# Transposes of q and k right behind the product of the first half pair, with a new order of the whole attention stage

## The chip, the cores and the metric

The kernel runs on one core of one Trainium2 chip. The metric is device time in microseconds (us), the median of several executions, lower is better. A profile is one more execution, recorded by the hardware. Five engines run side by side, each taking its own instructions in order: TensorE (PE, with its weight loads as PEld), VectorE (DVE), ScalarE (ACT), GpSimd (POOL) and SyncE (SP), which here only issues DMAs. Matrix products land in PSUM, eight banks of 512 float32 columns in each of 128 partitions.

## The reference

Attention in which a query sees only the keys of its own hash bucket, followed by a gated MLP:

```python
q_bits = (einsum(q, proj) > 0); k_bits = (einsum(k, proj) > 0)       # 6 bits each
mask   = q_bucket[:, :, :, None] == k_bucket[:, :, None, :]
scores = where(mask, (q @ k.T) / sqrt(64), -1e9); scores -= scores.max(-1)
x      = softmax(scores) @ v                 # batch 4, heads 8, seq 768, head_dim 64
h = gelu(x @ w_in); u, w = split(h); w = layernorm(w) * g_ln
out = x + (u * (w_sg @ w + b_sg)) @ w_out    # seq 768, d_model 512, d_ff 1024
```

## The kernel before

The 32 heads are worked on as 16 pairs: two heads of 64 rows fill the 128 partitions. The attention stage takes the pairs one after the other, and each pair in two halves of 384 queries. The MLP follows from about 422 us on. The numbers inside are float32; a product that must be exact is split into a high and a low part.

For a pair, the work on PE is made of these groups; the letter is used in the rest of the text.

- **T** (line 544, `parts`): six 128x128 transposes of q, and six of k, into a slot of two PSUM banks each. ACT copies each slot back over the raw tile (line 556, "x"), then makes the rounded part hq or hk (line 550, "hi"), and DVE the rest lq or lk (line 553, "lo"). The raw tiles have one buffer each, so the next pair's load waits until these are through. The T of pair n+2 are made while pair n is worked on.
- **F** (line 576): projections that give the hash bits of pair n+2. DVE takes their sign, and four DMAs put them into the tiles fq and fk.
- **M** (line 622, `largest`): 128 query rows against half of the keys, to find the largest score; four matmuls. DVE reduces the two banks to a maximum (line 627, "R"). Six M make a half.
- **S** (line 640, `shift`): three small transposes of the maxima, which ACT copies into a row of fq (line 646, "C", two copies per half). S and C are made one half ahead of the scores that use them.
- **W** (line 662, `weigh`): 128 keys against the 384 queries of a half, eight matmuls into a two-bank slot. ACT takes the exponential into a tile p (line 667, "E"). Six W make a half. POOL adds the p tiles up (line 676).
- **U** (line 716) sums over partitions, and **V** (line 692, `weighted`) is the product of six p tiles with v, 24 matmuls. ACT copies the result out (line 707, "un").

M and W use the array in two halves of 64 rows at once ("row"); U and F use it by 32 columns, V by 64 columns; T and S use it whole.

PE's order is not the order of the code. Each group is put down with an engine, an estimated cost and a priority (`Plan.add`). A planner (`Plan.order`) plays the engines through with its own costs and takes, when an engine is free, the ready group with the lowest priority number; PSUM slots are handed out on the way. The constants at the top and the table SHAPE shift the priorities, so changing them reorders every engine, and with it the slot that a group gets. A group whose slot was used before waits until the engine that reads the earlier contents is through. At most four two-bank slots exist, and U, V, F and S take single banks of the same eight.

Of the kernel before, what the change touches and what calls it, by code (L numbers as in the profile page):

```python
# [18 lines left out]
DRAM = bass.MemoryType.DRAM  # L19


MLP = {"xl": "POOL", "gm": "DVE", "gl": "POOL", "wg": 456.91, "wo": -41.91, "x": 458.24}

NSUM = 3
BANKED = False
HID = 304.61
AVP = 3.07
S0P = -1.32
AHEAD = 4
PREP, SHIFTP, FINP, WSTEP, WP = 10.15, -4.79, 9.31, 9.56, 22.97  # L30
LOADS = "SP"
GPLACE = 4
XLATE = 5.15
FIRST = -5
RXP = 9.55
FEAT = 2.68
LOWP = 7.25
LOADP = 2.29
LATF = 3.2
OM = [0.01, 0.27, 0.0, 2.44, 0.37, 0.0, -1.25, 0.68, 0.49, 1.13, -0.06, 0.0]  # L40
OW = [0.0, 0.2, 0.0, 0.29, 0.0, 0.0, 0.0, 0.0, -0.69, 0.48, 0.0, 1.07]
# [4 lines left out]
OH = [2.49, 0.0]  # L46
OT = [1.05, 0.73]
OF = [1.53, -2.21]
RATE = 2.72
WFROM = 1.22  # L50
ADDW = 2


SHAPE = {"A": [0.62, -1.19, 0.62, -0.38, 0.62, 1.31, 0.62, -1.1, 0.62, 0.62, 0.62, 0.62, -0.96, 0.62, 0.62, 0.62, 0.62, -2.07, 0.62, 0.62], "AV": [0.04, 0.0], "C": [3.79, 2.41, 3.53, 3.52], "E": [0.0, 0.0, -1.65, -0.24, 1.16, 0.0, -0.63, 2.51, 0.36, 0.0, -2.01, 0.0], "M": [0.0, 0.0, 0.0, 0.0, 0.0, -0.21, 0.0, 0.0, 0.0, -0.91, 0.0, -1.94], "R": [0.6, 0.6, 1.13, 0.6, -0.6, 0.6, 0.6, 0.44, 0.6, -1.08, 0.6, 0.6], "S": [0.18, 1.75], "T": [0.47, 0.68], "W": [0.0, 0.0, 0.0, 0.0, 0.0, 0.0, 0.0, 0.0, 0.0, 0.0, 0.0, 0.0], "hi": [3.88, -3.27], "lo": [0.0, -1.87], "m": [1.19, -3.45], "rc": [-3.68, 1.0], "sm": [4.69, -0.03], "un": [2.6, 6.46], "xt": [7.81, 0.51], "F": [-1.53], "sg": [-3.33], "x": [0.35, 1.9]}


class Plan:
# [46 lines left out]
    def add(self, engine, cost, prio, fn, r=(), w=(), dma=0, port=None, form=None, lat=0.0, tag=None):  # L104

        port = engine == "POOL" if port is None else port
        if tag in SHAPE:
            i = self.count[tag] = self.count.get(tag, -1) + 1
            prio += SHAPE[tag][i % len(SHAPE[tag])]
        if engine == "DVE" and port:  # L110
# [165 lines left out]
def kernel(  # L276
# [16 lines left out]
    nc = tc.nc  # L293

    B, H, S, D = q.shape
    P = 128
    NT = S // P
    HT = NT // 2
    SH = S // 2
# [112 lines left out]
    PE, DVE, ACT, POOL, SP = "PE", "DVE", "ACT", "POOL", "SP"  # L412
    xs = [dram.tile([DM, S], F32, name=f"xs_{b}") for b in range(B)]

    plan = Plan()
# [59 lines left out]
    if True:  # L475
# [5 lines left out]
        def ps_two():  # L481
            ps_s.list.append(plan.slot(ps_slots, 2, lambda i: psb[:, i:i + 2, :]))
            return ps_s.list[-1]
# [50 lines left out]
            st.ft = [f_tile(s, n % 2) for s in range(2)]  # L534
            return st

        def parts(st, s, prio):

            hh, lo, raw, fac, tp = st.hi[s], st.lo[s], st.raw[s], (SCALE, 1.0)[s], ps_two()

            def tr():
                for hf in range(2):
                    for i in range(HT):
                        nc.tensor.transpose(tp()[:, hf, i * P:(i + 1) * P],  # L544
                                            raw()[:, hf * HT + i].rearrange("p j d -> p (j d)"), ident)

            scale, fac = (fac, 1.0) if not st.n else (1.0, fac)

            def high():
                nc.scalar.mul(hh(), x_of(raw), fac)  # L550

            def low():
                nc.vector.scalar_tensor_tensor(lo(), x_of(raw), fac, hh().bitcast(F32), op0=ALU.mult, op1=ALU.subtract)

            plan.add(PE, 0.654, prio, tr, [raw], [tp], tag="T")
            plan.add(ACT, 0.81, prio, lambda: nc.scalar.mul(x_of(raw).rearrange("p (a b) -> p a b", a=2), tp()[:, :, :SH], scale), [tp], [raw], tag="x")
            def split(p1, p2):
                plan.add(ACT, 0.81, p1 + OH[s], high, [raw], [hh], tag="hi")
                if not st.n:
                    plan.add(POOL, 1.88, p2 + OL[s], lambda: nc.gpsimd.tensor_sub(lo(), x_of(raw), hh().bitcast(F32)), [raw, hh], [lo])  # L560
                    return
                plan.add(DVE, 0.98, p2 + OL[s], low, [raw, hh], [lo], port=True, tag="lo")

            st.split.append(split)

        def x_of(raw):
            return raw().rearrange("p t j d -> p (t j d)")
# [115 lines left out]
        def weighted(st, hf, prio, owed, nxt=None):  # L683

            av, p, v_ = ps_one(), st.p, st.v
            half = Pair()
            half.n, half.b, half.hp, half.hf, half.av, half.sum = st.n, st.b, st.hp, hf, av, st.sum

            def product():
                for kt in range(NT):  # L690
                    for j in range(2):
                        nc.tensor.matmul(av()[row(j), :SH + 1], v_()[:, j, kt, :], p[kt]()[:, j, :], start=(kt == 0), stop=(kt == NT - 1))  # L692

            if owed is None:
                plan.add(PE, 1.3 * HT, prio, product, p + [v_], [av], form="col")
            else:
                sums, tp = owed.sum, ps_one()

                def sumup():
                    total(sums, tp)  # L700
                    if nxt:
                        nxt.project()

                plan.add(PE, 0.35 + (0.66 if nxt else 0.0), prio - 0.02, sumup, p[-1:] + [sums] + (nxt.raw if nxt else []), [tp] + ([nxt.fp] if nxt else []), form="col32")
                plan.add(PE, 1.3 * HT, prio - 0.01, product, p + [v_], [av], form="col", tag="AV")
            half.un = un = late.ring([P, SH + 1], F32, "un", 3)
            plan.add(ACT, 0.48, prio - 1, lambda: nc.scalar.copy(un(), av()[:, :SH + 1]), [av], [un], tag="un")  # L707
            if owed is not None:
                finish(owed, tp, prio)
            return half  # L710
# [35 lines left out]
        NPAIR = B * NP  # L746
        sts = {}

        def prepare(n, prio):
            sts[n] = st = load(n, prio + LOADP)  # L750
            for s in range(2):
                parts(st, s, prio + 0.1 * s + OT[s])

        def loadv(st, prio):
            n = st.n
# [5 lines left out]
        def rest(st, prio):  # L761
            if st.n:
                st.sign(prio + OF[0])
                scatter(st, prio + OF[1])
            for s, f in enumerate(st.split):
                f(prio + XLATE + 0.1 * s, prio + LOWP + 0.1 * s)
            loadv(st, prio - 8)

        def maxima(i):
            n, t = divmod(i, NT)  # L770
            if n >= NPAIR:
                return
            p0 = 2 * (i - AHEAD) + S0P
            largest(sts[n], t, p0)
# [3 lines left out]
        owed = None  # L778
        for n in range(2):
# [3 lines left out]
            else:  # L783
                for s in range(2):
                    direct(sts[n], s, FIRST + 0.1 * s)
            rest(sts[n], (-12, -3)[n] + 0.3)
# [7 lines left out]
        for n in range(NPAIR):  # L794
            for c in range(NT):
                if c == 0 and n + 2 < NPAIR:
                    prepare(n + 2, 2 * (g_ := NT * n) + PREP)
                hf, k0, g = c // HT, 2 * (c % HT), NT * n + c
                maxima(g + AHEAD)
                weigh(sts[n], hf, k0, 2 * g)  # L800
                if c % HT == HT - 1:
                    nxt = sts.get(n + 2) if hf else None
                    if nxt:
                        features(nxt, 0, True)
                    owed = weighted(sts[n], hf, 2 * g + AVP + OA[hf], owed, nxt)
                    if nxt:
                        rest(nxt, 2 * g + FEAT)
                if c == 1 and GPLACE <= n < GPLACE + NT:
                    t = n - GPLACE
                    for h in range(P // Q):  # L810
                        c0 = t * P + h * Q
                        dma(2 * g + 20, 0.6, cost=0.85, fn=lambda eng, t=t, h=h, c0=c0: eng.dma_start(  # L812
                            wgd[t][h * Q:(h + 1) * Q].rearrange("b (f a) -> b f a", a=Q),
                            w_sg[:, c0:c0 + Q].rearrange("(f b) a -> b f a", b=Q)), r=[ticks[-1]], w=[(wgdb, (t, h))])
                while conv and WFROM + RATE * conv[0][0] <= 2 * g:
                    at_, job, args = conv.pop(0)
                    job(plan, w_tile, *args, 2 * g + WP, after=[ticks[-1]])
# [3 lines left out]

    M_ = MLP
    b1, b2 = Pool("b1", "right"), Pool("b2", "right")
# [160 lines left out]
    for b in range(B):  # L984
        p = 500 + 1000 * b
# [43 lines left out]
```

## Time and profile before

| | |
|---|---|
| three runs, us | 727.96, 728.36, 728.73 (median 728.36) |
| the profiled execution, us | 727.57 |
| its span, first to last instruction | 725.8 |
| granted TensorE clock over the span | 1.000 |
| busy share PE, DVE, POOL, ACT | 99%, 73%, 59%, 52% |

The profiled execution lies 0.79 us under the median of the three, and 1.8 us of it lie outside its span. A busy PE is not a PE that never waits: the ends of matmuls are modelled, and a wait of a tenth of a microsecond between two groups shows as a later start rather than as idle time. So the starts of successive groups are read here, not the busy share.

### The profile page before, as it was taken

The numbers are of one execution on the slowest core, as the hardware profiler recorded it, in microseconds if no ns is written. First come the engines' busy times: TensorE is split into PE (matmuls) and PEld (weight loads), VectorE is DVE, ScalarE is ACT, GpSimd is POOL, SyncE is SP. The second block draws the span as 40 slices with busy tenths as digits, with TensorE's granted clock in tenths as the row PEclk, the third lists the DMA queues.
The fourth block names the chain that finished last, engine by engine and source line by source line (L and its number), as shares of the span: only waits on it lengthen the run. The fifth ranks groups of instructions, "written<-read, shape, count | busy, mean of one in ns | idle before, by whom it ended". The sixth has DMA issues, their size and how long they took to land.

```text
span 725.8 us, 14083 instructions
## 1 busy us (share of the span) xinstructions
PE 715.9 (99%) x5294; PEld 565.4 (78%) x5294; DVE 528.9 (73%) x781; ACT 380.2 (52%) x611; POOL 430.9 (59%) x294
## 2 busy tenths in 40 slices
PE   8999999999999999999999999999999999999997
PEld 4676766767677676777767669988999899988995
DVE  6887788888998988888888359455953595349533
ACT  2675666657656565765656547422661275117410
POOL 4678787787877777596777848540562056304230
PEclk9999999999999999999999999999999999999999
DMA  6333652673665355346442236815130511051004
GB/s 130 85 66 92 149 119 87 133 155 100 151 150 138 96 111 140 87 126 156 103 113 60 60 113 193 174 39 119 30 88 29 116 30 45 15 131 30 0 1 117
DMA packets 177765, 70.38 MB, mean 97 GB/s; under 512 B 157728, under 2 KB 167968, under 8 KB 177696
## 3 DMA queue, kind: packets, MB, share of 16 engines
q1 hardware_dynamic: 176464, 68.62, 39.7%
q10 hardware_dynamic: 1232, 0.86, 0.5%
q8 instruction: 42, 0.69, 0.4%
q14 instruction: 27, 0.22, 0.1%
HBM read 51.61 MB, written 17.24 MB: 95 GB/s over the span
## 4 chain that ended last, share of the span: by engine, by line
PE 93%; DVE 3%; SPq 1%; DMA 1%; ACT 1%; issue 1%; DVEq 0%; ACTq 0%
PE psb L662 18%; PE psb L692 16%; PE psb L937 14%; PE psb L888 9%; PE psb L919 9%; PE psb L966 9%; PE psb L622 8%; PE psb L544 3%; DVE mx L627 2%; PE psb L716 2%; PE psb L576 1%; PE psb L640 1%; PE psb L455 1%; SPq L812 1%; DMA w<-in_moe_w_in_dram 0%
## 5 line engine op out<-in xcount | busy, mean ns | idle before, releaser
L676 POOL TENSOR_TENSOR sum<-sum,p 128x768 f32<-128x768 f32 x128 | 225.6, 1762 | 82.2 <-ACT p L667 74.5
L627 DVE TENSOR_REDUCE mx<-psb 128x2 f32<-128x768 f32 x192 | 175.9, 949 | 40.3 <-PE psb L622 38.5
L667 ACT ACTIVATE p<-psb 128x768 f32<-128x768 f32 x192 | 148.9, 814 | 29.4 <-PE psb L662 20.7
L692 PE MATMUL psb<-p,v 128*64 128x385 f32 x768 | 131.2, 491 | 0.0
L692 PEld LDWEIGHTS psb<-p,v 128*64 128x64 f32 x768 | 52.3, 137 | 71.7 <-issue 62.7
L662 PE MATMUL psb<-hq,hk 64*128 64x384 f32 x384 | 72.1, 371 | 1.1 <-DVE mx L627 0.6
L622 PE MATMUL psb<-fk,fq 64*128 64x384 f32 x384 | 66.9, 343 | 1.5 <-DVE mx L627 1.0
L676 POOL TENSOR_TENSOR sum<-p,p 128x768 f32<-128x768 f32 x32 | 61.2, 1914 | 11.7 <-ACT p L667 11.6
L622 PE MATMUL psb<-hk,hq 64*128 64x384 f32 x384 | 65.1, 333 | 0.0
L662 PE MATMUL psb<-lq,hk 64*128 64x384 f32 x384 | 65.0, 333 | 0.0
L662 PE MATMUL psb<-fq,fk 64*128 64x384 f32 x384 | 64.9, 333 | 0.0
L662 PE MATMUL psb<-hq,lk 64*128 64x384 f32 x384 | 64.8, 332 | 0.0
L948 POOL TENSOR_TENSOR gs<-gt,gs 128x384 fp32r<-128x384 f32 x32 | 33.6, 1054 | 52.0 <-ACT gs L945 47.2
L937 PE MATMUL psb<-wgh,zh 128*128 128x384 f32 x192 | 64.1, 334 | 0.0
L937 PE MATMUL psb<-wgl,zh 128*128 128x384 f32 x192 | 64.1, 334 | 0.0
L937 PE MATMUL psb<-wgh,zl 128*128 128x384 f32 x192 | 64.1, 334 | 0.0
L898 POOL TENSOR_TENSOR mv<-mv,epsr 128x1 f32<-128x1 f32 x24 | 13.2, 549 | 85.2 <-DVE mv L897 65.7
L872 ACT ACTIVATE h<-psb 128x384 f32<-128x384 f32 (+1 forms) x56 | 29.2, 534 | 65.8 <-PE psb L888 60.3
L707 ACT COPY un<-psb 128x385 f32<-128x385 f32 x32 | 15.4, 481 | 90.1 <-PE psb L692 90.1
L966 PE MATMUL psb<-woh,gs 128*128 128x512 f32 x192 | 59.9, 389 | 0.0
L873 DVE SCALAR_TENSOR_TENSOR h<-h,psb 128x384 f32<-128x384 f32 (+1 forms) x56 | 32.9, 603 | 28.4 <-ACT h L872 28.3
L940 DVE TENSOR_TENSOR gt<-psb,b_bc 128x384 f32<-128x384 f32 x32 | 17.8, 555 | 47.3 <-PE psb L937 43.7
(122 smaller groups left out, 1552.7 us busy)
## 6 DMA issues: line engine op xcount, KB each, us to landing
q<-in_q_dram SPq DMA_DIRECT2D x32, 192.0 KB
v<-in_v_dram SPq DMA_DIRECT2D x16, 384.0 KB
rs<-r SPq DMA_DIRECT2D x64, 96.0 KB
xs<-xt SPq DMA_DIRECT2D x32, 192.0 KB
x<-xs SPq DMA_DIRECT2D x16, 384.0 KB
rx<-xs SPq DMA_DIRECT2D x96, 64.0 KB
out_dram<-ob SPq DMA_DIRECT2D x24, 256.0 KB
k<-in_k_dram SPq DMA_DIRECT2D x31, 192.0 KB
```

Source lines behind the costliest of these rows:

```text
L622: nc.tensor.matmul(sc[kh]()[:, j, :SH], x[0]()[row(j), qs], x[1]()[row(j), kh * SH:(kh + 1) * SH], start=(n == 0), stop=(n == 1))
L627: plan.add(DVE, 0.95, prio + OM[2 * t + kh], lambda kh=kh: nc.vector.tensor_reduce(mx()[:, i, :, kh], sc[kh]()[:, :, :SH], axis=AX.X, op=A ...
L662: nc.tensor.matmul(sc[i]()[:, j, :SH], x()[row(j), ks], y()[row(j), cs], start=(n == 0), stop=(n == 3))
L667: plan.add(ACT, 0.81, prio, lambda i=i: nc.scalar.activation(p[i]()[:, :, :SH], sc[i]()[:, :, :SH], AF.Exp), [sc[i]], [p[i], ticks[-1]], t ...
L676: plan.add(POOL, 1.88, prio + 0.6, lambda i=i, first=first: nc.gpsimd.tensor_add(sums(), (first or sums)()[:, :, :SH], p[i]()[:, :, :SH]), ...
L692: nc.tensor.matmul(av()[row(j), :SH + 1], v_()[:, j, kt, :], p[kt]()[:, j, :], start=(kt == 0), stop=(kt == NT - 1))
L873: plan.add(DVE, us + 0.07, prio, lambda: nc.vector.scalar_tensor_tensor(h2()[:, :n], h2()[:, :n], 1.0 / GA, ps()[:, :n], op0=ALU.add, op1= ...
L888: nc.tensor.matmul(ps(), x()[:, ts_], w[:, c, FH:FF], start=(c == 0 and n == 0), stop=(c == NC - 1 and n == 2))
L919: nc.tensor.matmul(ps()[:, :SH], w[:, c, fs], x()[:, cs], start=(c == 0 and n == 0), stop=(c == NC - 1 and n == 2))
L937: nc.tensor.matmul(vp()[:, :SH], z()[:, t, fs], w()[:, t, cs], start=(t == 0 and n == 0), stop=(t == NT - 1 and n == 2))
L948: nc.gpsimd if e == POOL else nc.vector).tensor_sub(gl()[:, cs], gt(), gh()[:, cs].bitcast(F32)),
L966: nc.tensor.matmul(po(), a()[:, ts_], w()[:, f, :], start=(f == 0 and n == 0), stop=(f == NF - 1 and n == 2))
```

## The change

The T of q and k no longer belong to `prepare` (except for the first two pairs). They are put down in the main loop right behind the product V of a pair's first half, and a marker buffer, written by V and read by T, forbids them to come earlier. Constants and SHAPE have new values, and with them the order of all engines. Line numbers behind the first edits move by 1 to 7; line 662 becomes 663, 622 becomes 623, 544 becomes 545.

```diff
-HID = 304.61
+HID = 266.96
+TP = -6.37
-PREP, SHIFTP, FINP, WSTEP, WP = 10.15, -4.79, 9.31, 9.56, 22.97
+PREP, SHIFTP, FINP, WSTEP, WP = 2.53, -5.4, 9.46, 2.63, 22.15
...
-        def parts(st, s, prio):
+        def parts(st, s, prio, behind=()):
...
-            plan.add(PE, 0.654, prio, tr, [raw], [tp], tag="T")
-            plan.add(ACT, 0.81, prio, lambda: nc.scalar.mul(x_of(raw).rearrange("p (a b) -> p a b", a=2), tp()[:, :, :SH], scale), [tp], [raw], tag="x")
+            plan.add(PE, 0.654, prio, tr, [raw, *behind], [tp], tag="T")
+            plan.add(ACT, 0.81, prio + (OT[s] - TP if behind else 0.0), lambda: nc.scalar.mul(x_of(raw).rearrange("p (a b) -> p a b", a=2), tp()[:, :, :SH], scale), [tp], [raw], tag="x")
...
-                plan.add(PE, 1.3 * HT, prio - 0.01, product, p + [v_], [av], form="col", tag="AV")
+                half.mark = plan.buf("mark", 1000)
+                plan.add(PE, 1.3 * HT, prio - 0.01, product, p + [v_], [av, half.mark], form="col", tag="AV")
...
             sts[n] = st = load(n, prio + LOADP)
-            for s in range(2):
-                parts(st, s, prio + 0.1 * s + OT[s])
+            if n < 2:
+                for s in range(2):
+                    parts(st, s, prio + 0.1 * s + OT[s])
...
                     if nxt:
                         rest(nxt, 2 * g + FEAT)
+                    elif not hf and n + 2 < NPAIR:
+                        for s in range(2):
+                            parts(sts[n + 2], s, 2 * g + TP + 0.1 * s, [owed.mark])
```

PE in the program before, the tenth pair, from the end of V of its first half (p and v are V's operands, identr and m those of S, the rest W and M):

```order
L692 MATMUL psb<-p_160,v_2880 64x385 x2
L640 MATMUL psb<-identr,m_71 66x128 x3
L662 MATMUL psb<-hq_4_2853,hk_4_2832 128x384 x2
L662 MATMUL psb<-hq_4_2853,lk_4_2864 128x384 x2
L662 MATMUL psb<-lq_4_2882,hk_4_2832 128x384 x2
L662 MATMUL psb<-fq_177,fk_178 128x384 x2
L622 MATMUL psb<-fk_176,fq_175 128x384 x2
L622 MATMUL psb<-hk_5_3144,hq_5_3168 128x384 x2
```

Here S follows V at once, then the first W and M. Some 20 rows later on PE before, the two T (operand ident) stand between an M and a W:

```order
L622 MATMUL psb<-fk_176,fq_175 128x384 x2
L622 MATMUL psb<-hk_5_3144,hq_5_3168 128x384 x2
L544 MATMUL psb<-ident,k_3198 128x128 x6
L544 MATMUL psb<-ident,q_3213 128x128 x6
L662 MATMUL psb<-hq_5_3168,hk_5_3144 128x384 x2
L662 MATMUL psb<-hq_5_3168,lk_5_3178 128x384 x2
```

They part a run of M and W here. PE in the changed program, the same place behind V:

```order
L693 MATMUL psb<-p_160,v_2879 64x385 x2
L545 MATMUL psb<-ident,q_3215 128x128 x6
L545 MATMUL psb<-ident,k_3204 128x128 x6
L641 MATMUL psb<-identr,m_71 66x128 x3
L663 MATMUL psb<-hq_4_2841,hk_4_2801 128x384 x2
L663 MATMUL psb<-hq_4_2841,lk_4_2855 128x384 x2
L663 MATMUL psb<-lq_4_2876,hk_4_2801 128x384 x2
L663 MATMUL psb<-fq_177,fk_178 128x384 x2
```

Both T moved from the run of M and W to the place between V and S. This half's order is V S W M W M W M M W M T T W W M U F V before and V T T S W M W M W M M W M W W M U F V after, alike in all 14 pairs for which the change makes T.

ACT in the program before, from the copy un behind the same V (fq is C, p is E, k and q are x, hk and hq are hi):

```order
L707 COPY un_3326<-psb 128x385
L646 CAST fq_175<-psb 1x384 x2
L667 ACTIVATE p_163<-psb 128x2x384
L667 ACTIVATE p_164<-psb 128x2x384
L667 ACTIVATE p_165<-psb 128x2x384
L667 ACTIVATE p_166<-psb 128x2x384
L556 ACTIVATE k_3198<-psb 128x768
L556 ACTIVATE q_3213<-psb 128x768
```

Here x comes when four E are through. ACT in the changed program from the same copy on:

```order
L710 COPY un_3324<-psb 128x385
L557 ACTIVATE q_3215<-psb 128x768
L557 ACTIVATE k_3204<-psb 128x768
L647 CAST fq_175<-psb 1x384 x2
L668 ACTIVATE p_163<-psb 128x2x384
L668 ACTIVATE p_164<-psb 128x2x384
L668 ACTIVATE p_165<-psb 128x2x384
L668 ACTIVATE p_166<-psb 128x2x384
L551 ACTIVATE hk_5_3423<-k_3204 128x768
```

The two copies x moved from behind the fourth E to the place ahead of C and of the first E. PE's rows of the MLP and of the last pairs stand in the order that they had.

## Rows read from the trace of the kernel before

**Rows 1.** The page: busy time by engine, and the chain that ended last.
```profile
PE 715.9 (99%) x5294; PEld 565.4 (78%) x5294; DVE 528.9 (73%) x781; ACT 380.2 (52%) x611; POOL 430.9 (59%) x294
...
PE 93%; DVE 3%; SPq 1%; DMA 1%; ACT 1%; issue 1%; DVEq 0%; ACTq 0%
```

**Rows 2.** The chain of waits: pieces of V (start us, us, what).
```profile
30.89 4.03 PE psb L692 x24
...
311.49 4.03 PE psb L692 x24
325.11 4.03 PE psb L692 x24
336.61 4.03 PE psb L692 x24
...
387.69 4.03 PE psb L692 x24
```

**Rows 3.** Timeline of PE around the two T (start us, us, line, operation).
```profile
269.46 0.34 PE L622 MATMUL psb<-hk,hq 64*128 64x384 f32 x2
269.73 0.88 PE L544 MATMUL psb<-ident,k 128*128 128x128 f32 x6
270.44 0.83 PE L544 MATMUL psb<-ident,q 128*128 128x128 f32 x6
271.21 0.44 PE L662 MATMUL psb<-hq,hk 64*128 64x384 f32 x2
271.49 0.34 PE L662 MATMUL psb<-hq,lk 64*128 64x384 f32 x2
```

**Rows 4.** Timeline of PE behind V of the same half.
```profile
264.63 0.40 PE L640 MATMUL psb<-identr,m 128*66 128x128 f32 x3
...
266.12 0.35 PE L662 MATMUL psb<-hq,hk 64*128 64x384 f32 x2
...
266.81 0.35 PE L622 MATMUL psb<-fk,fq 64*128 64x384 f32 x2
...
267.16 0.35 PE L662 MATMUL psb<-hq,hk 64*128 64x384 f32 x2
```

**Rows 5.** Timeline of ACT in the same half (in brackets idle time before, and its releaser).
```profile
265.13 0.94 ACT L646 CAST fq<-psb 1x384 fp32r<-1x384 f32 x2
266.10 1.75 ACT L667 ACTIVATE p<-psb 128x768 f32<-128x768 f32 x2
268.14 0.81 ACT L667 ACTIVATE p<-psb 128x768 f32<-128x768 f32 x1 [0.29 <-PE psb L662]
...
270.64 0.81 ACT L556 ACTIVATE k<-psb 128x768 f32<-128x768 f32 x1 [0.29 <-PE psb L544]
271.35 0.81 ACT L556 ACTIVATE q<-psb 128x768 f32<-128x768 f32 x1
```

**Rows 6.** Timeline of ACT behind V of another pair.
```profile
162.97 0.64 ACT L405 ACTIVATE wih<-wx 128x512 fp32r<-128x512 f32 x1 [4.09 <-DVE wx L404]
...
164.84 1.51 ACT L667 ACTIVATE p<-psb 128x768 f32<-128x768 f32 x2
```

**Rows 7.** Timeline of PE in the same stretch.
```profile
165.70 0.44 PE L662 MATMUL psb<-hq,hk 64*128 64x384 f32 x2 [0.21 <-ACT p L667]
165.99 0.34 PE L662 MATMUL psb<-hq,lk 64*128 64x384 f32 x2
```

**Rows 8.** Timeline of SP: loads of q, and copies of w_sg.
```profile
0.74 1.03 SPq L528 DMA_DIRECT2D q<-in_q_dram  x2
...
153.16 1.43 SPq L528 DMA_DIRECT2D q<-in_q_dram  x2
...
155.96 3.83 SPq L812 DMA_DIRECT2D wgd<-in_moe_w_sg_dram  x4
```

**Rows 9.** Timeline of PE: the first T, and V of the pair with those copies.
```profile
6.26 0.88 PE L544 MATMUL psb<-ident,q 128*128 128x128 f32 x6
...
158.33 0.87 PE L692 MATMUL psb<-p,v 128*64 128x385 f32 x4
```

More of the change, by code (lines that the diff above doesn't have):

```diff
@@ L19 @@
 DRAM = bass.MemoryType.DRAM
-MLP = {"xl": "POOL", "gm": "DVE", "gl": "POOL", "wg": 456.91, "wo": -41.91, "x": 458.24}
+MLP = {"xl": "POOL", "gm": "DVE", "gl": "POOL", "wg": 473.46, "wo": 4.34, "x": 593.02}
 NSUM = 3
 BANKED = False
-HID = 304.61
+HID = 266.96
 AVP = 3.07
+TP = -6.37
 S0P = -1.32
 AHEAD = 4
-PREP, SHIFTP, FINP, WSTEP, WP = 10.15, -4.79, 9.31, 9.56, 22.97
+PREP, SHIFTP, FINP, WSTEP, WP = 2.53, -5.4, 9.46, 2.63, 22.15
 LOADS = "SP"
 GPLACE = 4
[L33 to L38, printed above, removed]
+XLATE = 4.54
+FIRST = -12.81
+RXP = 12.47
+FEAT = -0.09
+LOWP = 1.4
+LOADP = 2.48
 LATF = 3.2
@@ L48 @@
 OF = [1.53, -2.21]
-RATE = 2.72
+RATE = 2.75
 WFROM = 1.22
 ADDW = 2
-SHAPE = {"A": [0.62, -1.19, 0.62, -0.38, 0.62, 1.31, 0.62, -1.1, 0.62, 0.62, 0.62, 0.62, -0.96, 0.62, 0.62, 0.62, 0.62, -2.07, 0.62, 0.62], "AV": [0.04, 0.0], "C": [3.79, 2.41, 3.53, 3.52], "E": [0.0, 0.0, -1.65, -0.24, 1.16, 0.0, -0.63, 2.51, 0.36, 0.0, -2.01, 0.0], "M": [0.0, 0.0, 0.0, 0.0, 0.0, -0.21, 0.0, 0.0, 0.0, -0.91, 0.0, -1.94], "R": [0.6, 0.6, 1.13, 0.6, -0.6, 0.6, 0.6, 0.44, 0.6, -1.08, 0.6, 0.6], "S": [0.18, 1.75], "T": [0.47, 0.68], "W": [0.0, 0.0, 0.0, 0.0, 0.0, 0.0, 0.0, 0.0, 0.0, 0.0, 0.0, 0.0], "hi": [3.88, -3.27], "lo": [0.0, -1.87], "m": [1.19, -3.45], "rc": [-3.68, 1.0], "sm": [4.69, -0.03], "un": [2.6, 6.46], "xt": [7.81, 0.51], "F": [-1.53], "sg": [-3.33], "x": [0.35, 1.9]}
+SHAPE = {"A": [-2.08, -3.89, -2.08, -3.08, -2.08, -1.39, -2.08, -5.91, -2.08, -2.08, -1.54, -2.08, -3.66, -2.08, -2.08, -2.08, -2.08, -4.81, -2.08, -2.08], "AV": [0.34, 0.0], "C": [3.92, 2.22, 3.66, 3.36], "E": [-0.14, -1.21, -1.67, -0.26, 4.83, -0.02, -1.26, 2.31, 0.34, -1.96, -0.33, -0.02], "M": [0.0, 0.0, 0.0, 0.0, 0.0, -0.3, 0.0, 0.0, 0.0, -0.91, 0.0, -1.94], "R": [0.46, 0.46, 0.99, 0.46, -0.74, 0.31, 2.58, -0.97, 0.46, 0.57, 0.46, 1.52], "S": [1.1, 2.78], "T": [-0.95, -0.94], "W": [0.0, 0.0, 0.0, 0.0, 0.0, 0.0, 0.0, 0.0, 0.0, 0.0, 0.0, 0.0], "hi": [7.69, -2.1], "lo": [0.0, -1.87], "m": [0.12, -3.45], "rc": [-3.68, 3.73], "sm": [-2.98, -4.2], "un": [-1.1, 4.87], "xt": [9.75, 3.26], "F": [-2.57], "sg": [-5.71], "x": [-2.69, 0.29]}
 class Plan:
@@ L694, in weighted @@
             if owed is None:
-                plan.add(PE, 1.3 * HT, prio, product, p + [v_], [av], form="col")
+                half.mark = plan.buf("mark", 1000)
+                plan.add(PE, 1.3 * HT, prio, product, p + [v_], [av, half.mark], form="col")
             else:
@@ L704, in weighted @@
                 plan.add(PE, 0.35 + (0.66 if nxt else 0.0), prio - 0.02, sumup, p[-1:] + [sums] + (nxt.raw if nxt else []), [tp] + ([nxt.fp] if nxt else []), form="col32")
-                plan.add(PE, 1.3 * HT, prio - 0.01, product, p + [v_], [av], form="col", tag="AV")
+                half.mark = plan.buf("mark", 1000)
+                plan.add(PE, 1.3 * HT, prio - 0.01, product, p + [v_], [av, half.mark], form="col", tag="AV")
             half.un = un = late.ring([P, SH + 1], F32, "un", 3)
```

## The prediction

> **What bounds the kernel now.** First the page: PE is busy 99% of the span, no other engine over 73%, and the chain that ended last lies on PE for 93% [rows 1]. So time goes where PE's groups start later, and it comes back where they start earlier. Next the pieces of V in the chain of waits [rows 2]. From the V at 30.89 to the one at 387.69 lie 14 pairs in 356.80 us, 25.49 us each. The pair from 311.49 to 336.61 took 25.12, and its half from 311.49 to 325.11, the one that holds the T, 13.62, of which 4.03 is V and 9.59 the rest. Were every pair as short, the 14 would take 351.7: about 5.1 us of the stage are waits that come and go from pair to pair. Then the timeline of PE where the change takes something out [rows 3] and puts it in [rows 4], and the timeline of ACT there [rows 5], since ACT empties the T.
>
> **What goes.** A T in the middle of a run of M and W costs more than its matmuls. The two matmuls of the last M step are at 269.46, and steps of M and W are 0.17 apart (266.81 to 267.16 is one M of two steps, 0.35) [rows 4], so the next would have come at 269.63. T of k came at 269.73: 0.10 for leaving the run. The two T took 0.71 and 0.77, to 271.21. The first step of W then took 0.28 instead of 0.17: 0.11 for coming back [rows 3]. From 269.63 to 271.21, with that 0.11, the break cost 1.69 us. Behind V there is no run to break: V is followed by a whole-array group (S) before and after, and the W behind S pays for its change of form either way. There I take 0.71 for each T, the step from one T to the next [rows 3]. No row shows T followed by S; above it is bounded by the longest step from a T, 0.77, and I allow as much below, 0.65. So 1.42 in place of 1.69: 0.27 us saved per pair, 3.8 us in 14 pairs.
>
> **What comes: ACT.** T must be emptied, and in the new order both copies x stand ahead of C, and C ahead of the first E. Times from the end of V, for one half:
> - T of q at 0, T of k at 0.71. A copy x starts 0.91 behind the start of its T (269.73 to 270.64) [rows 3, 5], so at 0.91; the second starts 0.71 later (270.64 to 271.35) [rows 5], at 1.62, and C another 0.71 later, at 2.33.
> - From C to the first E 0.97 (265.13 to 266.10), and E lasts 0.81 [rows 5]. The first E ends at 4.11. A PE group that waits for it starts some 0.05 later (164.84 plus 0.81 is 165.65, the W starts at 165.70) [rows 6, 7]: at 4.16.
> - PE: before, the third W stood 2.53 behind the end of V (264.63 to 267.16) [rows 4]. With two T ahead it could start at 3.95. But of the eight banks T holds four, S one, and by then the second W and the second M have taken what x and C gave back; the third W gets the slot of the first W and needs its E. It waits 0.21. A W that waited also loses its early weight load: its first step takes 0.29 instead of 0.17 (165.70 to 165.99) [rows 7], 0.11 more. Together 0.32.
> - The sixth W gets the slot of the fourth. Between them lie W, M and W, 0.69 plus 0.35 plus 0.69, 1.73 [rows 4]. E starts 0.98 behind its W (267.16 to 268.14) [rows 4, 5]; with 0.81 and 0.05 the slot comes free at 1.84. A wait of 0.11, and again 0.11 for the weights: 0.22. Before, the two T lay in between and hid it.
>
> Together 0.54 a pair, 7.6 us in 14. The first two M and the second W, whose slots x and C give back, find them through: x of q ends at 1.72, the first M starts at 2.56 (0.35 ahead of the second W); x of k ends at 2.43, the second W starts at 2.91; the second C ends at 3.27, the second M starts at 3.60 [rows 4, 5]. ACT has no slack to do x earlier, as T can only be read when V is over.
>
> Such a chain did occur before. In one pair a weight conversion of 0.64 us stood ahead of un, C and E, and the third W behind S started only at 165.70, released by E [rows 6, 7]. That is the wait that the new order builds into every pair.
>
> By the Trainium skill, "Perfetto Trace Analysis", section "Identifying the Most-Contended Engine", one optimizes the engine of the highest occupancy first. By that alone ACT at 52% would be no bound here, and the change would keep its whole saving. The same page, section "Optimization Strategy", says that a gap repeating on the engine that should be saturated can mean too little PSUM for the next tile; by that the saving is lost. The rows of the late half bear out the second, in one half; no run shows it yet in every pair.
>
> **What comes: the rest.** In one pair ACT's new order has a weight conversion between C and E; it is 0.64 long [rows 6], of which I count 0.5, as ACT starts each copy 0.1 before the end of the last (0.81 long, 0.71 apart) [rows 5]: 0.5 us more, once. In one pair the load of q stands behind the four w_sg copies on SP. Before, q was issued there until 154.59, the copies until 159.79 [rows 8]. With q behind them its issue ends at about 159.8. Landing takes at most 4.5 from the end of issue (issued by 1.77, T at 6.26) [rows 8, 9], so 164.3 at the latest. In that pair V ends at 162.4 (158.33 plus 4.03) and T of q, the second, is due 0.71 later, at 163.1 [rows 2, 9]. A wait between 0 and 1.2, and I take the middle, 0.6. In all other pairs the loads stand well ahead of V on SP, and I cost them at nothing; one that is late costs what that pair's does. The hi and lo copies move among the E and R; V, 4.03 us in which no new score comes, covers them [rows 2], and without it each would cost about an x, 0.8 [rows 5]. MLP, U, F and V: the same groups, 0.
>
> **Sum.** Minus 3.8 plus 7.6 plus 0.5 plus 0.6 is 4.9 us on the profiled 727.57, which gives 732.5. The median of the runs lies 0.79 above that execution, so the sum against it is 733.3. A little of the new wait will fall into stalls of DVE that are there already, so I say 733.0. The bounds of the terms: T 0.65 to 0.77 (1.7 us both ways over 28 T), the load 0 to 1.2, and each wait on E 0 to 0.1 longer, 2.8 us; 731 to 736 together.
>
> **Rivals.**
> - The gain stays. If the third and sixth W do not wait (E earlier by 0.2 is enough, or the slot was free), 3.8 us go: 724.6. For it: ACT is idle nearly half the span. Against: the sum of ACT's steps leaves 0.2 too little in each pair, each step from a row. The point from which it decides is the end of the first E: before 3.9 us behind V, or after. Chance 0.14.
> - Nothing to measure. The 5.1 us of waits that come and go [rows 2] shrink in the new order about as much as the waits on E cost: 728.4. For it: nearly every constant of the order is new. Against: these waits are few and uneven, and the order of M and W within the first half is unchanged but for the T. Chance 0.13.
> - DVE becomes the bound. The pause of 1.5 us that the T gave the reductions R in mid run is gone. If the changing waits double, 5.1 us more: 738. For it: the run of M and W has no other pause. Against: the pause is now in front of the run, where DVE can do its conversions. Chance 0.12.
> - The forecast, waits on E in every pair, 731 to 736. Chance 0.61.
>
> **Numbers.** 733.0 is the likeliest. Below 727.0 lies most of the first rival, above 737.0 half of the third: the range is 727.0 to 737.0. About 0.2%, 1.5 us, is what a measurement of this kernel can tell from no change. Faster by more than that takes the first rival and a little of the second, 0.15; the same is the rest of the second and a little of the forecast, 0.13; slower 0.72.
>
> **What would show it.** In the timeline of PE of the changed kernel: V, T, T, S, W without a gap, and no step of 0.10 or 0.11 around T; then the third W behind S with an idle time released by E (the list of waits has W behind E many times instead of twice), and its first step 0.28. On ACT un, x, x, C, C, E without a gap, with the first E ending 4.1 behind V. The half with the T takes about 13.9 from V to V, the other half as long as before. I am wrong if the third W starts 3.95 behind V, or if that half takes 13.4; the DVE rival is right if the waits on R, not on E, grow.

## The result, and the profile after

The changed kernel takes 734.96 us (median of five runs, 732.80 to 737.74) against 728.22 for the kernel before on the same chip (726.93 to 728.73): a ratio of 1.0089, 95% interval 1.0068 to 1.0111. It is slower, by 6.7 us; the forecast was 733.0, with a range of 727 to 737. The profiled execution after took 733.33, 1.6 below that median; its span is 731.5 at a granted clock of 0.999, against 725.8 before.

The page, busy time by engine and the chain that ended last:

```profile
PE 716.9 (98%) x5294; PEld 565.6 (77%) x5294; DVE 529.6 (72%) x781; ACT 378.9 (52%) x611; POOL 434.3 (59%) x294
...
PE 87%; DVE 5%; ACT 3%; DMA 2%; issue 1%; SPq 1%; DVEq 0%; ACTq 0%
```

Against [rows 1] the work is the same (PE within 1.0 us, the other engines within 3.4), but the chain that ended last has left PE for 6% of the span: 2% more on DVE, 2% on ACT, 1% on DMA. The whole is a matter of who waits for whom.

The pieces of V in the chain of waits (start us, us, what), as in [rows 2]:

```profile
262.32 4.03 PE psb L693 x24
276.20 4.03 PE psb L693 x24
301.65 4.03 PE psb L693 x24
313.15 4.03 PE psb L693 x24
328.18 4.03 PE psb L693 x24
```

From here on a half is the time from one V to the next, numbered by the V that begins it; odd halves from 1 to 27 hold the T, in both programs. The half from 262.32 takes 13.88 where a usual one took 13.62 [rows 2], the one from 301.65 is one without T (11.50), and the one from 313.15 takes 15.03. Read from the starts of all V on PE:

| us | first V | median half with T | 14 halves with T | 14 without | last V to the end |
|---|---|---|---|---|---|
| before | 30.82 | 13.69 | 194.7 | 162.1 | 307.7 |
| after | 31.35 | 13.89 | 198.4 | 164.2 | 307.2 |

The three halves 29 to 31, which the table leaves out, take 30.4 in both. So the 5.7 us of span lie in the stage that the change orders: 3.6 in the halves with T, 2.1 in those without; 0.5 ahead of the first V and minus 0.5 from the last V on cancel. Regular is the 0.20 in each half with T: 2.8 in 14. The rest is not regular. After, halves 8, 23, 25 and 28 take 12.61, 15.03, 16.33 and 12.64, together 5.8 over the medians (13.89, and 11.50 without T); before, no half was over 14.82. Over all 28 halves the excess over the medians is 7.0 after and 4.1 before.

The timeline of PE at the place of [rows 3, 4], from the end of V on (start us, us, line, operation; in brackets idle time before, and its releaser):

```profile
266.28 0.87 PE L545 MATMUL psb<-ident,q 128*128 128x128 f32 x6
266.99 0.82 PE L545 MATMUL psb<-ident,k 128*128 128x128 f32 x6
267.57 0.43 PE L641 MATMUL psb<-identr,m 128*66 128x128 f32 x3
267.92 0.45 PE L663 MATMUL psb<-hq,hk 64*128 64x384 f32 x2
...
269.77 0.36 PE L623 MATMUL psb<-fk,fq 64*128 64x384 f32 x2
269.94 0.36 PE L623 MATMUL psb<-hk,hq 64*128 64x384 f32 x2
270.47 0.44 PE L663 MATMUL psb<-hq,hk 64*128 64x384 f32 x2 [0.17 <-ACT p L668]
270.75 0.34 PE L663 MATMUL psb<-hq,lk 64*128 64x384 f32 x2
```

And ACT behind the same V:

```profile
266.40 0.48 ACT L710 COPY un<-psb 128x385 f32<-128x385 f32 x1 [2.82 <-PE psb L693]
267.24 0.81 ACT L557 ACTIVATE q<-psb 128x768 f32<-128x768 f32 x1 [0.36 <-PE psb L545]
267.95 0.81 ACT L557 ACTIVATE k<-psb 128x768 f32<-128x768 f32 x1
268.64 0.94 ACT L647 CAST fq<-psb 1x384 fp32r<-1x384 f32 x2
269.60 1.51 ACT L668 ACTIVATE p<-psb 128x768 f32<-128x768 f32 x2
```

That is the chain of the prediction, x, x, C, C, E without a gap; only between un and the first x does ACT wait, 0.36 for T. The first E ends at 269.60 plus 0.81, 4.13 behind the end of V at 266.28 (forecast 4.11), the third W starts at 4.19 (forecast 4.16), with an idle time that E releases, and its second step comes 0.28 later instead of 0.17.

What W (line 663) and M (line 623) waited for, over the whole kernel, from the view of one line (us, times; a weight load and the matmul behind it are both counted, so the sums are not time of the span). After:

```profile
  DVE mx L628: 9.3, 21
  ACT p L668: 9.0, 31
```
```profile
  DVE mx L628: 10.1, 18
  ACT p L668: 1.2, 4
```

The first pair of lines is W's, the second M's. Before, W waited 3.8 in 13 places for E and 5.4 for R, and M 5.0 for R. So both kinds of wait grew: the forecast's (E, line 668) and a rival's (R, line 628). In the list of waits of PE alone, without the weight loads, W behind E goes from the first of these lines to the second:

```profile
PE psb L662 <- ACT p L667: 0.4, 2, 0.2
```
```profile
PE psb L663 <- ACT p L668: 1.4, 8, 0.2
```

Eight, not 14. Read half by half, the third W is released by E in halves 1, 3, 9, 13, 15, 17, 19 and 23, at 4.14 to 4.19 behind V. In 5, 7, 11, 21 and 27 R releases it, at 4.09 or 4.10, and in 25 too, at 5.29. The experiments part the two.

### The profile page after: what moved, and what is told of

Same layout as the page of the kernel before. It is cut to its first block, busy times and chain, and to the rows that moved or that the text cites. A ratio compares the mean times of both kernels' runs of the same rounds, so it can differ in the third digit from the quotient of the medians.

```text
span 731.5 us, 14106 instructions
## 1 busy us (share of the span) xinstructions
PE 716.9 (98%) x5294; PEld 565.6 (77%) x5294; DVE 529.6 (72%) x781; ACT 378.9 (52%) x611; POOL 434.3 (59%) x294
## 4 chain that ended last, share of the span: by engine, by line
PE 87%; DVE 5%; ACT 3%; DMA 2%; issue 1%; SPq 1%; DVEq 0%; ACTq 0%
PE psb L663 16%; PE psb L693 15%; PE psb L944 14%; PE psb L895 9%; PE psb L926 9%; PE psb L973 9%; PE psb L623 7%; DVE mx L628 3%; PE psb L545 3%; PE psb L719 2%; ACT p L668 1%; PE psb L577 1%; PE psb L641 1%; DMA sq<-s 1%; ACT fq L647 1%
## 5 line engine op out<-in xcount | busy, mean ns | idle before, releaser
L677 POOL TENSOR_TENSOR sum<-p,p 128x768 f32<-128x768 f32 x32 | 64.6, 2020 | 11.7 <-ACT p L668 11.7
```

The costliest lines, as they stand in the source:

```text
L677: plan.add(POOL, 1.88, prio + 0.6, lambda i=i, first=first: nc.gpsimd.tensor_add(sums(), (first or sums)()[:, :, :SH], p[i]()[:, :, :SH]), ...
```

## The experiments

Theory A is the prediction's: x, x and C ahead of E make the third and sixth W wait. Theory D grew with the trace after: R, the reduction of M, comes late, because DVE has other work in front of it. Each kernel was timed against the kernel before on the same chip; the ratios are to that, with 95% intervals.

### 1. The place of T alone

```diff
 PE, the half behind V of a pair's first half
- V S W M W M W M M W M T T W W M
+ V T T S W M W M W M M W M W W M
 ACT
- un C C E E E E x x E E
+ un x x C C E E E E E E
```

> The kernel before with its own table of numbers; only the two T of a pair are put right behind V, ahead of S, on ScalarE the two x ahead of the two C, and the PSUM buffers of that half are handed round as in the changed kernel. Nothing else moves: DVE, POOL and the DMA queues keep the order of before. Theory A (the place of T is what costs: ScalarE's row x, x, C, C, E ends later, and the third W and the sixth W then wait for a buffer): a half that holds T takes 13.8 to 13.9 us against 13.65 in the trace of before, 14 of them give 2 to 3.5 us: 730 to 732 us. Rival B (the place saves its 0.41 us in each pair, and the cost of the changed kernel comes from the new order that its table gives to DVE, POOL and the loads): the halves take 13.25 us, 14 x 0.41 = 5.7 us less than before: 722 to 724 us.

Measured: 761.38, ratio 1.0459 (1.0436 to 1.0481). Both were far off. The halves with T did as theory A says, 13.90 in the median. But the halves without T went from 11.50 to a median of 13.29, and their sum from 162.1 to 193.3. The view of DVE in one of them (start us, us, line, operation):

```profile
152.42 0.17 DVE L695 TENSOR_REDUCE m<-mx 128x6 fp32r<-128x18 f32 x1
...
153.12 2.53 DVE L613 SCALAR_TENSOR_TENSOR lk<-k,hk 128x768 fp32r<-128x768 f32 x1
155.57 2.59 DVE L613 SCALAR_TENSOR_TENSOR lq<-q,hq 128x768 fp32r<-128x768 f32 x1
158.09 2.05 DVE L801 SCALAR_TENSOR_TENSOR xt<-un,rs 128x384 f32<-128x384 f32 x1
160.06 1.89 DVE L462 TENSOR_SCALAR wy<-wx 128x512 int32<-128x512 int32 x1
161.87 1.81 DVE L687 TENSOR_REDUCE mx<-psb 128x2 f32<-128x768 f32 x2
```

POOL and PE in the same stretch:

```profile
153.02 1.81 POOL L736 TENSOR_TENSOR sum<-p,p 128x768 f32<-128x768 f32 x1
154.80 2.55 POOL L904 TENSOR_TENSOR xl<-x,xh 128x768 fp32r<-128x768 f32 x1
157.95 7.30 POOL L736 TENSOR_TENSOR sum<-sum,p 128x768 f32<-128x768 f32 x4 [0.60 <-ACT p L727]
```
```profile
162.87 0.44 PE L682 MATMUL psb<-fk,fq 64*128 64x384 f32 x2 [3.25 <-DVE mx L687]
...
163.87 0.53 PE L722 MATMUL psb<-lq,hk 64*128 64x384 f32 x2
164.19 0.53 PE L722 MATMUL psb<-fq,fk 64*128 64x384 f32 x2
```

The same instructions in the kernel before:

```profile
147.66 1.70 DVE L553 SCALAR_TENSOR_TENSOR lk<-k,hk 128x768 fp32r<-128x768 f32 x1
149.28 2.57 DVE L553 SCALAR_TENSOR_TENSOR lq<-q,hq 128x768 fp32r<-128x768 f32 x1
151.77 0.60 DVE L741 SCALAR_TENSOR_TENSOR xt<-un,rs 128x384 f32<-128x384 f32 x1
152.30 0.41 DVE L402 TENSOR_SCALAR wy<-wx 128x512 int32<-128x512 int32 x1
153.25 1.82 DVE L627 TENSOR_REDUCE mx<-psb 128x2 f32<-128x768 f32 x2 [0.54 <-PE psb L622]
```

```profile
148.51 2.53 POOL L844 TENSOR_TENSOR xl<-x,xh 128x768 fp32r<-128x768 f32 x1
153.27 1.70 POOL L676 TENSOR_TENSOR sum<-sum,p 128x768 f32<-128x768 f32 x1 [2.23 <-ACT p L667]
```

xt takes 2.05 instead of 0.60 and wy 1.89 instead of 0.41, while POOL adds up p tiles at 157.95; before, POOL was idle from 151.04 to 153.27. An R runs in 0.95 each either way. So lk to wy, 5.1 us before, take 8.8, the first R starts 10.4 behind the start of V instead of 6.4, and M waits 3.25 for its buffer. T behind V sets this off in two ways: the E of its half, and with them POOL's sums, come later (in the half ahead of this one the first sum behind E is 8.31 behind the start of V, and was 6.45), so POOL still adds the last p tiles when DVE makes lk, which takes 2.53 instead of 1.70; and the run of M has lost its pause, so m is 0.8 later. With both, xt begins 6.59 behind the start of V instead of 4.96, and so meets the next sums, which stand at 6.46 as before. Over the kernel lk takes 2.53 in the median, and 1.79 before. The old order of DVE's work did not fit the new place. With the new table of numbers the same place costs 6.7 us, without it 34.

A part of the 34 is PE's clock. Right behind that wait of 3.25 the granted clock is 0.50, the lower of its two levels (1.2 GHz), from 163.5 to 166.5, and steps of M and W take 0.32 instead of 0.17. That adds 1.6 to half 10, which takes 16.38 instead of 11.51: the wait and these 1.6. The clock falls twice more, at the end of waits for R of 3.10 and 3.17 in halves 12 and 18; by the lengthened steps it is some 6 us in the three halves (an estimate). From 30 us to the last V it stays at 1.00 in the kernels before and after.

### 2 and 3. The copies x made short, after and before

```diff
-nc.scalar.mul(x_of(raw).rearrange("p (a b) -> p a b", a=2), tp()[:, :, :SH], scale)
+nc.scalar.mul(x_of(raw).rearrange("p (a b) -> p a b", a=2)[:, :, :8], tp()[:, :, :8], scale)
```

> The changed kernel, in which the copies x of the transposed q and k move 8 of 384 columns of each bank; most of the transposed q and k is left out of what follows. The order is that of the changed kernel on every engine. Theory A: with each x shorter by about 0.5 us, the exponentials of the half come 0.9 us sooner, the third W no longer waits (0.35 us more than a step without a wait, 8 to 14 times), and the sixth less: 3 to 6.5 us less than the changed kernel, 728.5 to 732. Rival B (DVE, POOL and the loads): no change, 734 to 736.

> The kernel before with the same shortened copy x (the same part left out). There x stands in the middle of the exponentials, behind the fourth. Theory A: no W waits long for an exponential in that kernel, so nothing is won: 727 to 728.5 us. Rival C (the copies x cost the same wherever they stand, ScalarE is simply full): as much is won as in the changed kernel, 3 to 6 us: 722 to 725.

Measured: after with short x 735.17, ratio 1.0117 (1.0089 to 1.0144), so no gain over the changed kernel; before with short x 726.29, ratio 0.9988 (0.9979 to 0.9997). The time of the first contradicts theory A, its trace does so in part. W and M's waits in it, as above:

```profile
  DVE mx L628: 14.0, 26
  ACT p L668: 3.8, 15
```
```profile
  DVE mx L628: 14.5, 23
```

W waits for E 3.8 in 15 places, as before the change, instead of 9.0 in 31. In the eight halves in which E released the third W it now starts 3.83 to 3.86 behind V, without a wait; in the others R releases it, at 4.09 or later. The halves that are then free of R, 1, 3 and 9, take 13.49, 13.55 and 13.53, less than any half with T before. But 5, 13, 15, 17, 19, 21 and 27 take 13.76 to 13.82, as M and W wait for R a little further on, and the waits for R grew by 9 us (weight loads counted too, as above). Halves 23 and 25 take 17.46 and 18.02: at the end of waits for R of 2.18 and 2.54 the granted clock falls and is 0.50 from 323.6 to 326.9 and from 350.9 to 354.2, and the steps of 0.32 add some 3 us in the two. What E gave back, R and the clock took, and more. That before gains only 0.9 speaks against rival C: x costs where it stands ahead of E.

### 4. S ahead of T

```diff
 PE
- V T T S W
+ V S T T W
 ACT
- un x x C C E
+ un C x x C E
```

> The changed kernel with S ahead of the two T, and on ScalarE one C ahead of the two x and one behind them: C, x, x, C in place of x, x, C, C. Everything else stays. Theory A: the 0.36 us for which ScalarE waits for the first T are filled by a C, the exponentials start 0.1 to 0.4 us sooner, and the third W waits as much less: 1.5 to 5 us less than the changed kernel, 730 to 733.5. Rival B: no change, 734 to 736.

Measured: 732.77, ratio 1.0081 (1.0066 to 1.0096): not to be told from the changed kernel by its time. In the trace the time from the start of the second M to the third W falls from 0.68 in the median to 0.53 (0.35 before the change), and W waits 7.0 in 25 places for E instead of 9.0 in 31: theory A's direction. The median half gains only 0.06, from 13.89 to 13.83, as other steps of it became a few hundredths longer; halves 23 and 25 stay at 14.98 and 16.35.

### 5, 6 and 7. The conversion of w_in made short: after, before, and with T's place alone

```diff
+        N8 = CW if th is None else 8
...
-        plan.add("POOL", 0.14 + CW / 512, prio, lambda: nc.gpsimd.tensor_mul(g(), hi().bitcast(F32), hi().bitcast(F32)), [w], [g])
+        plan.add("POOL", 0.14 + CW / 512, prio, lambda: nc.gpsimd.tensor_mul(gg(), hi().bitcast(F32), hi().bitcast(F32)), [w], [g])
...
-        vec(lambda: sts(xf(), g(), LEAST * LEAST, xf(), op0=ALU.is_ge, op1=ALU.mult), [x, g], [x])
+        vec(lambda: sts(xf(), gg(), LEAST * LEAST, xf(), op0=ALU.is_ge, op1=ALU.mult), [x, g], [x])
...
```

Here hi, lo, xf and gg give the first N8 columns of their tiles, 8 of 512 for w_in.

> The changed kernel with its order on every engine, in which the conversion of w_in works on 8 of 512 columns in four of its seven DVE steps and in its POOL product, and takes one tensor less in a fifth; most of that conversion is left out. Theory D (what is lost beyond 0.2 us in each half with T is DVE: a conversion or a low half stands between m and the first R of a half, is stretched beside a POOL sum, and R comes late): the halves that wait for R through w_in's conversion become regular, the halves with T go to 13.8, 3 to 5 us less than the changed kernel: 729.5 to 732. The halves of 15.0 and 16.3 us, which belong to w_out, stay. Rival A (all of it is ScalarE and the place of T): no change, 734 to 736.

> The kernel before with the same conversion left out, its order unchanged. Theory D: the halves of 14.2 to 14.8 us that have w_in's conversion ahead of R lose some 0.5 us each: 725 to 727. Rival A: no change, 727.5 to 728.5.

> The first of the experiments (the kernel before, T alone put behind V) with the same conversion left out. Theory D: its extra 33 us are R behind DVE's work of before, which no longer fits; with most of that work gone the halves without T return to 11.5 to 12.5 us, the halves with T stay at 13.9: 729 to 740. Rival E (the extra time comes from something else that the move does, a load or a buffer): 755 to 762.

Measured: after 731.43, ratio 1.0066 (1.0048 to 1.0083); before 725.85, 0.9987 (0.9976 to 0.9998); T's place alone 740.43, 1.0187 (1.0168 to 1.0206). The last is the decisive one, though it lies a little above the 729 to 740 expected: the same work taken from DVE (and one product from POOL) is worth 0.9 us in the order of before and 20 us with T alone moved (1.0459 to 1.0187, times 727). Its halves without T fall from 193.3 in sum to 173.4, its halves with T stay at 13.90. Some 4 of the 20 are clock, as it now falls once, at the end of a wait for R of 2.99 in half 10, and not three times. So most of the first experiment's loss is theory D, with the clock that falls behind its longest waits, and the regular 0.2 is not. (Of the 14 us that are left to 726.5, some 2 lie in the halves with T, which add up to 196.4; most of the others lie in halves without T, where lk, lq and xt still stand ahead of R. 1.6 of them are the clock in half 10; the rest was not taken apart.) No run changes POOL's sums alone: that it is their overlap, and not DVE's queue by itself, that makes R late is read from the rows above. In the changed kernel the gain is smaller than expected, and its interval overlaps that of the changed kernel; halves 23, 25 and 28 stay at 14.70, 16.06 and 12.63, since what stands in front of R there is w_out's conversion and the pair's own lk, lq and xt.

### 8 and 10. DVE's order mended in the changed kernel

DVE in half 25 of the changed kernel, the worst:

```profile
347.57 0.43 DVE L399 TENSOR_SCALAR wy<-w 128x512 int32<-128x512 int32 x1 [1.88 <-DMA wo_h<-wy]
347.91 0.95 DVE L628 TENSOR_REDUCE mx<-psb 128x2 f32<-128x768 f32 x1
348.78 1.94 DVE L400 SCALAR_TENSOR_TENSOR wx<-w,wy 128x512 int32<-128x512 int32 x1
350.64 0.94 DVE L628 TENSOR_REDUCE mx<-psb 128x2 f32<-128x768 f32 x1
```

And PE in the same half:

```profile
348.92 0.44 PE L663 MATMUL psb<-hq,hk 64*128 64x384 f32 x2 [0.74 <-DVE mx L628]
351.64 0.44 PE L663 MATMUL psb<-hq,hk 64*128 64x384 f32 x2 [1.05 <-DVE mx L628]
```

A conversion step waits 1.88 for the store of the piece before it (its tile wy is being written to DRAM), and the first R stands behind it; the next step is stretched to 1.94 beside POOL and holds up the second R. Each edit puts such steps behind R's; for half 25, in the tenth experiment:

```diff
 DVE, half 25 (c: a step of w_out's conversion)
- m c c c R c R R R R R
+ m c c c R R R R R c R
```

One of the four c of before is in the next half, behind lk and lq; the first c of the new row comes from half 24.

> The changed kernel with six instructions of DVE put later: in the halves of 12.61, 15.03, 16.33 and 12.64 us (8, 23, 25 and 28) the normalising xt and the conversion steps that stand ahead of R go behind the R's. Nothing else moves but two stores behind xt. Theory D: the R's are on time, these four halves lose 0.6 to 1.1, 1.2, 2.4 and 1.1 us: 5 to 6 us less than the changed kernel, 729 to 730.5. Rival A: no change, 734 to 736.

> The changed kernel with DVE's order mended as in the eighth experiment, but with the conversion steps of halves 23 and 25 in the next half, behind the low halves, where DVE is idle, not ahead of m: the table of signs fc, and the features that are scattered from it, are then no longer late. Theory D: 8, 23, 25 and 28 come to 11.5, 13.9, 13.9 and 11.5 us and 24 stays at 11.5: 5 to 6 us less than the changed kernel, 2 to 3 over before, a ratio of 1.002 to 1.004: what is left is the 0.2 us in each of 14 halves with T. Rival A: as the changed kernel, 1.008 to 1.009.

Measured: the eighth 733.10, ratio 1.0081 (1.0062 to 1.0100), the tenth 730.16, 1.0047 (1.0028 to 1.0065). The eighth's trace is that of its fastest execution, 730.86, so its halves add up to more gain than its median has. In it, halves 8, 23 and 28 fell as said, to 11.52, 13.88 and 11.36, half 25 to 15.56. But half 24 rose from 11.49 to 13.41. A conversion step put ahead of m made m, xt and the signs fc late, and M waited for the features made of them:

```profile
333.38 0.45 PE L631 MATMUL psb<-fk,fq 64*128 64x384 f32 x2 [1.55 <-DMA fk<-fc]
```

In the tenth, with the steps behind lk and lq instead, half 24 takes 11.48, half 23 13.88 and half 28 11.30. Half 25 still takes 15.08: now ACT's share of the late conversion stands ahead of un and x, and M waits 0.60 for x of q. Half 26 takes 12.89: a step put there was stretched in its turn, to 2.18, and R came late again, as the row of PE below shows. Halves 4 and 29, with 12.30 and 12.14, are 0.8 and 0.65 longer than in the changed kernel, too.

```profile
362.02 0.44 PE L671 MATMUL psb<-hq,hk 64*128 64x384 f32 x2 [1.15 <-DVE mx L636]
```

Still, some 3 of the 6.7 us came back by moving a dozen instructions that touch neither T nor E; W's waits for E stay, 9.6 in 32 places. By theory A alone nothing would have come back.

### 11. Both mended

```diff
 PE, ACT: as in experiment 4; DVE: as in experiment 10
 PSUM
- sixth W: slot of the fourth W (free after its E);  last M: slot of an M (free after its R)
+ the two slots exchanged
```

> The one above, with S ahead of the two T and C, x, x, C on ScalarE (as in the fourth), and with the PSUM buffers of the sixth W and the M behind it exchanged, so that the sixth W waits for an R instead of an exponential. Theories A and D together: the third W waits 0.15 us less and the M behind the sixth W stops losing its 0.11 us, 14 x 0.2 = 2 to 3 us less than the one above, level with the kernel before: a ratio of 0.998 to 1.001. If the waits of the third and sixth W cost nothing, as the one above: 1.002 to 1.004.

Measured: 729.81, ratio 1.0041 (1.0028 to 1.0054), not to be told from the tenth. W's waits for E are down to 6.2 in 20 places, and seven of the halves with T take 13.69 to 13.75, against 13.62 to 13.71 in eight of them before. But half 11 takes 15.11, with T waiting 0.41 for the load of q that stands behind the four w_sg copies, and half 25 15.41. Most of the regular cost is gone in those halves; others became irregular.

### 9 and 12. DVE's order mended in the kernel before

Four halves of the kernel before, 7, 11, 21 and 27, take 14.24 to 14.82, each with a conversion step ahead of R. If order of DVE is all, it should be faster still.

```diff
 DVE, half 21 (c: a step of w_in's conversion)
- m c c c c R R R R R xt R | m fc lk lq c
+ m c c c R R R R R xt R | m fc lk lq c c
```

> The kernel before, T in its old place, with four steps of its weight conversion put later: in the halves of 14.33, 14.82, 14.24 and 14.46 us (7, 11, 21, 27) the DVE step that stands just ahead of the first R (in 11 and 27 with ScalarE's share of that conversion, which stands among the exponentials) goes behind the R's. Nothing else moves but two loads and stores that belong to these steps. Theory D, for the kernel before too: these halves lose 0.5 to 1.1 us each, 2 to 3.1 us less than before: a ratio of 0.9957 to 0.9973. Rival A (the place of T decides, DVE's order is free): no change, 0.999 to 1.001.

> The kernel before, T in its old place, mended anew: in halves 11, 21 and 27 the conversion step just ahead of the first R goes into the next half, behind its two low halves, not ahead of m (which in the ninth experiment made m, the signs and the features late), ScalarE's share goes behind the exponentials, and the next conversion's first steps go behind that half's R's. Half 7 is left as it is, so no load of weights moves. Theory D: halves 11, 21 and 27 lose 0.9, 0.4 and 0.8 us and no other half gains: 2 us less than before, a ratio of 0.9965 to 0.998. If what is put later always comes back in a later half, as in the ninth: 1.000 to 1.008.

Measured: the ninth 733.04, ratio 1.0078 (1.0052 to 1.0104); the twelfth 727.89, 1.0014 (1.0002 to 1.0026). The six times of the ninth run from 730.33 to 735.40, and its trace is that of the slowest. In both, the halves that were mended fell as said, in the ninth to 13.62, 13.91, 13.81 and 13.67, in the twelfth 11, 21 and 27 to 13.89, 13.84 and 13.62. In both, it came back elsewhere: in the ninth in half 9 (16.02, an E behind a copy on ACT that waited for a load), 12 (13.46) and 28 (15.04); in the twelfth in half 9 (14.28), 13 (15.03) and 29 (12.54). One row of PE of the twelfth, in half 29, where a late step of the conversion stands ahead of the last R and so of m:

```profile
391.68 0.37 PE L648 MATMUL psb<-identr,m 128*66 128x128 f32 x3 [1.00 <-DVE m L643]
```

The kernel before stands in a narrow place: none of the kernels that do the whole work is faster than it.

## Why the prediction was right, and where it was not

- **In range, in part by luck.** The forecast was 4.9 us on the profiled execution, and 5.7 were measured. Of its 4.9, 3.8 were to be a regular cost in each pair; that came out as 2.8. The other 2.9 measured are excess in single halves, most of it behind R, for which the sum had only the two single terms, 1.1 together. Two misses of opposite sign brought the time near 733.
- **What goes: 0.27 a pair.** Too small. The break of [rows 3] is the usual one: over the halves with T it cost 1.69 in the median. Behind V, T, T and S take 0.71, 0.57 and 0.35, where S alone took 0.33: 1.31. Saved: 0.38 a pair. The step from T to S is 0.57 in all 14 pairs, not 0.71, and outside my bounds of 0.65 to 0.77, which came from T followed by W or T.
- **What comes: 0.54 a pair.** Right in size, 0.58 in the median (the 0.38 saved and 0.20 lost), and the mechanism held, but not in every pair. Where E releases the third W, in eight halves, it starts 4.14 to 4.19 behind V (4.16 said). As T and S are shorter than I took, it could have started at 3.84 and not 3.95, so it waits 0.35, not 0.21, and with 0.11 for the weights the cost is 0.46, not 0.32: what the shorter T saved was lost again at the same E. In the other six R releases it: there its slot is not that of the first W, as I had it for every pair. For the sixth W and the M behind it I said 0.22; in the half of the rows it was 0.19. It is released by E in ten halves, by R in three, and does not wait in one. Experiments 1, 2 and 4 move the third W as they should. But experiment 2 shows that R stands close behind E: without the wait for E only three halves came below those of before.
- **The two single terms, 0.5 and 0.6.** The pair with the conversion between C and E has a half of 14.19, 0.3 over the median. The load behind the w_sg copies made no T wait in the changed kernel (no step between two T is over 0.78): q's issue ended at 161.43 there, later than the 159.8 that I gave, but T of q was due only at 164.75. It is close, though: in experiments 2, 10 and 11 a T of that pair waited 0.21, 0.17 and 0.41 for it.
- **"A little of the new wait will fall into stalls of DVE that are there already."** This step failed, and with it the reason that I gave against the third rival, that DVE can do its conversions in the pause in front of the run. There POOL is still adding, as its p tiles come 1.9 later, and lk, xt and wy take 1.5, 3.4 and 4.6 times as long in the half read in experiment 1. Experiments 1 and 7 show that this is by far the larger effect of the new place (the halves without T lost 31 of the 33 us of span, some 6 in all through the clock, and 20 came back when DVE's conversion was cut), and that the new order, which I had costed at nothing, takes most of it back. What it leaves over is what the forecast lacks: 5.8 us in four halves, against 3.1 over the median in halves 7, 11, 21 and 27 of before. R, not E, sets most of the excess there: experiment 10 takes back some 3 us by DVE's order alone.
- **The rivals.** "The gain stays" would have been right in three halves without the wait for E: the halves of 13.5 in experiment 2 are 0.1 to 0.2 below the same halves of before. "DVE becomes the bound" was right in part: by my own sign, the waits on R, both kinds grew. In PE's list of waits those for R went from 2.4 to 5.7 us, 3.3 more where I gave that rival 5.1, and those of W for E from 0.4 to 1.4.

What stays open is how much of the excess of single halves belongs to which step: each mended half sent some of it on to another, so the runs give the sum and not a price for each. Nor does a run show how far another table of numbers could bring the new place down.

## What to carry to other kernels

- Where three engines feed each other through a few buffers, a group moved on one engine moves the others in time; here it was the overlap of DVE and POOL that cost most. Look at what will run beside what after the move, before counting the steps of the moved engine.
- A step that ends late on an engine that takes its work in order costs what is queued behind it. In front of the instruction that frees a buffer, put nothing that waits for a DMA and nothing that a neighbour can stretch, and look where it goes instead: in experiments 8 to 12 a part of it came back in a later half.
- A time that agrees with the forecast can hold a mechanism that the forecast lacks: read the single long stretches too, not only the median one.

## What the runs showed of the hardware

In these traces DVE's instructions with two operands in SBUF, and some with one, can take several times as long while POOL works; those that read PSUM do not. The views of one line, of before for xt and after for R (duration ns min/median/max, first and last start, form):

```profile
L741 DVE SCALAR_TENSOR_TENSOR xt<-un,rs x32: 601/1151/2127, 67.0 to 442.2; 128x384 f32<-128x384 f32 x32
```
```profile
L628 DVE TENSOR_REDUCE mx<-psb x192: 908/951/962, 12.1 to 405.0; 128x2 f32<-128x768 f32 x192
```

The same xt takes 0.60 to 2.13 us, an R 0.91 to 0.96 in 192 places, and m, a small reduction from SBUF, 0.13 to 0.18 in 32. Where POOL was idle beside it, xt took 0.60 or 0.61 (10 of its 32 places before). The Trainium skill, "SBUF — State Buffer", section "Who interferes with whom", says that a DVE instruction with two SBUF inputs contends with a GpSimd instruction that reads SBUF, and that the port pair that the two share is an exclusive lock. The runs agree, with 0.60 against 2.05 for xt: in experiment 1 it began 0.14 behind a sum of POOL and ended 0.42 behind that sum's end. By the same section a form of one SBUF operand can contend too, in some modes; here wy took 0.41 with POOL idle and 1.89 beside its sums.

Six transposes followed by S cost 0.57 us in all 14 halves after, followed by six more 0.71, though each is the same six matmuls. No run shows why.

The granted clock of TensorE fell from 1.00 to 0.50 (2.4 to 1.2 GHz) in the attention stage of three traces, each time at the end of a wait of PE for R, of 2.2 to 3.3 us: three times in experiment 1, twice in experiment 2 and once in experiment 7. Such a wait cost some 1.5 us more than its own length, in half 18 of experiment 1 about 2.8.
